# A linear-attention and gated-unit kernel in float32: plain out products for two batches, another load order, a new plan

## The chip, the cores and the metric

The kernel runs on one core of one Trainium2 chip. The metric is device time in microseconds; the time before is the median of three runs, and the profile is of one further execution.

## The reference

Eight batches, eight heads, 576 tokens, head size 64. All arithmetic is float32; three weights arrive as float64 and are narrowed on the chip.

```python
kv = np.einsum('bhsd,bhse->bhde', k, v)
out = np.einsum('bhsd,bhde->bhse', q, kv)
rms = np.sqrt(np.mean(out * out, axis=-1, keepdims=True) + 1e-06)
x = out / rms * g_norm                      # then (B,H,S,D) -> (B,S,512)
for t in range(5):
    gate_pre += conv_w[t] * xp[:, t:t + S, :]   # causal taps over tokens
gate = 1.0 / (1.0 + np.exp(-gate_pre))
return (gate * (x @ w_val)) @ w_out
```

## The kernel before, in words

The work goes batch by batch, and each batch has five stages.

**Attention.** `kv_product` (L400) makes the 64x64 products of k and v, a pair of heads to a step, from two half loads of each (`load_half`, L257) and from tails of 64 tokens (`load_tails`, L266). `kv_copy` (L415) puts them on the diagonal of `kvbd`. q has to stand with the head's elements on the partitions: the first two batches turn it on TensorE (`turn_q_rows`, L439, then `sort_q`, L452), the others on VectorE (`turn_q`, L425). `raw_product` (L478) multiplies both for one chunk of 128 tokens (a last chunk has 64). The norm is `square` on ScalarE, `sums` on VectorE, `powers` (exponent -0.5) on GpSimd and `normalise` on VectorE. x is then turned: on TensorE for the first two batches (`turn_x`, L528, `keep_x`), by VectorE and DMA for the others (`turn_blocks`, `move_blocks`).

**Gates.** Four strips of 128 channels in a batch: `gate_start` on ScalarE, four `gate_tap` (L569) on VectorE, and a sigmoid. **Val.** x @ w_val in float32: batches 0 to 3 in plain form (`val_product`, L580, 32 steps), the others in a form with seven block products in place of eight (`val_fast`, L619). `gated` multiplies val by the gate into `gv`, which has room for three batches.

**Out.** gv @ w_out, by pairs of batches (i). In a batch two groups p of two chunks of 128 tokens each use seven block products in place of eight: `fast_product` (L703) has 7 steps of two matmuls each, 128x128 by 256 columns. They need sums of weights (`weight_sums`, once) and of tokens (`token_sums`, L682, four VectorE operations for each batch), and seven `fast_keep` (L725) collect the banks: four ScalarE copies and three VectorE adds. The last 64 tokens of both batches of a pair form one chunk more, made by `out_product` (L658) in plain form with 64-wide weights, and `keep_out` (L670). `store` (L746) issues four transfers for each chunk.

**Weights.** Each of nine pieces (four of w_val, four of w_out, conv_w) is loaded (`stage_weight`) and narrowed in eight steps (`narrow_weight`), five on VectorE and three on ScalarE.

What sets the order: nothing is scheduled at run time. `Planner` (L52) is given every step with an engine, a duration, a due time (`want`), what it needs and which ring of buffers it takes; `SHIFTS` (L21) moves due times of single kinds and batches. `order` (L103) takes again and again the step that can start first, ties by due time, and the steps are recorded in that order. Each engine runs its own instructions in that order, and waits by semaphores for the others. The loads stand in SP's queue likewise: at most eight transfers are under way, since each takes one of eight semaphores in turn. Before a TensorE step of the first 60 us of the plan, `keep_warm` (L392) puts matmuls of the identity (L397) into the time that the plan has free; they write to a spare half of the bank that holds kv. The PSUM rings are kv 1, raw 2, tp 1 and mm 4 banks; `kv_copy` reads the same bank as the keep-warm matmuls write.

Of the kernel before, what the change touches and what calls it, by code (L numbers as in the profile page):

```python
# [15 lines left out]
P = 128  # L16
# [2 lines left out]


SHIFTS = {  # L21
    "fast_keep": {3: 8},
    "fast_product": {1: -15, 3: -3.5},
    "gate_tap": {0: 30, 1: 40.5, 2: 66, 3: 64, 4: 72.5, 5: 53, 6: 56, 7: 32.5},
    "kv_product": {2: 48.5, 5: 19.5},
    "load_half": {("k", 0): -105.5, ("k", 3): 4.5, ("k", 4): -12, ("k", 6): -27.5, ("v", 0): -11.5,
        ("v", 4): -13, ("v", 5): -11, ("v", 7): -9.5},
    "load_q": {2: -6, 5: 2, 6: -30, 7: -22},
    "load_q_rows": {0: -16},
    "load_tails": {4: -1.5, 5: 0.5, 7: -0.5},  # L30
    "move_blocks": {3: 22.5},
    "narrow_weight": {("wout", 1): 6, ("wout", 2): 6, ("wout", 3): 7.5, ("wval", 0): -19,
        ("wval", 1): -26.5, ("wval", 2): 14},
    "normalise": {2: 12, 7: -20},
    "out_product": {1: -28},
    "raw_product": {4: -1.5},
    "stage_weight": {("cw", 0): -102, ("wout", 1): 30.5, ("wout", 2): 7, ("wout", 3): 57, ("wval", 1): 3,
        ("wval", 2): -109, ("wval", 3): -93},
    "sums": {2: 16.5, 3: -3.5, 4: -37.5, 5: 11.5, 7: 24.5},
    "token_sums": {0: -31.5},  # L40
    "turn_blocks": {6: -13, 7: 1},
    "turn_q": {2: 16.5, 3: 11.5},
    "turn_x": {1: 11.5, 6: 14},
    "val_fast": {4: 38, 7: 9},
    "val_keep": {6: -64},
    "val_product": {0: 11, 1: 10.5, 2: 34.5, 3: 34.5},
    "val_sums": {1: 41},
    "x_sums": {6: 16},
}


# [85 lines left out]
def kernel(  # L137
# [37 lines left out]
    nc = tc.nc  # L175
    B, H, S, D = q.shape
    C = H * D
    HP = H // 2
    NJ = S // P
    SF = NJ * P  # L180
    T = S - SF
    NK = C // P
# [8 lines left out]
    TURNED = 2  # L191
    TURNED_X = 2
    FAST_VAL = range(4, B)
    GATES = 3
    GVS = 3
    assert NJ == 4 and NB == 18
# [24 lines left out]
    gv = const.tile([P, NK, GVS * S], FP32, name="gv")  # L221
# [5 lines left out]
    cw = const.tile([NK * K, P], FP32, name="cw")  # L227
    cwT = const.tile([P, K, NK], FP32, name="cwT")
    wval = const.tile([P, NK, C], FP32, name="wval")
    wout = const.tile([P, NK, C], FP32, name="wout")  # L230
# [427 lines left out]
    def out_product(i, c):  # L658

        po = ps("mm", [P, C], f"out{i}_{c}")  # L660
        for jt in range(NK):
            for r in range(2):
                first = (2 * i + r) % GVS * S + SF
                nc.tensor.matmul(  # L664
                    po[r * T:(r + 1) * T], gv[:, jt, first:first + T], wout[:, jt, :],
                    start=(jt == 0), stop=(jt == NK - 1),
                )
        st["po", i, c] = po
# [287 lines left out]
    def gated_all(*batches):  # L956
        return [("gv", (b, jt)) for b in batches for jt in range(NK)]

    def single(b, first):

        key = b // 2, 2 * NJ
        plan.add(
            "PE", 3.6, first, out_product, *key,
            needs=gated_all(b - 1, b) + [("wout", jt) for jt in range(NK)],
            gives=[("po", key)], takes=[("mm", ("po", key))], frees=[("gv", b - 1), ("gv", b)],
        )
        plan.add(
            "ACT", 0.5, first + 3.6, keep_out, *key, needs=[("po", key)], gives=[("ot", key)],
            takes=[("ot", key)], frees=[("mm", ("po", key))],
        )  # L970
        plan.add(
            "SP", 2.0, first + 4.3, store, *key, needs=[("ot", key)], frees=[("ot", key)],
            load=0.26 / RATE,
        )

    def outputs(b, first):

        i, h = divmod(b, 2)
        used = gated_all(b)
        for n in range(4):  # L980
            plan.add(
                "DVE", 0.62, first - 4.0 + n, token_sums, i, h, n,
                needs=used + ([("sums", (i, h, n - 1))] if n else []), gives=[("sums", (i, h, n))],
                takes=[("w64", ("sums", i, h, n // 2))] if n % 2 == 0 else [],
            )
        for m in range(2):
            p = 2 * h + m
            t = first + 6.2 * m
            for n in range(7):
                key = i, p, n  # L990
                last = (i, p, n - 1) if n else (i, p - 1, 6) if p else None
                own = {2: 0, 4: 2, 5: 1, 6: 4}.get(n)
                own_sums = {1: 0, 2: 1, 4: 2, 5: 3}.get(n)
                plan.add(
                    "PE", 0.9, t + 0.88 * n, fast_product, *key,
                    needs=used + ([("fast", last)] if last else [])
                    + ([("kept", (i, p, own))] if own is not None else [])
                    + ([("sums", (i, h, own_sums))] if own_sums is not None else [])
                    + ([("wsum", 3)] if n not in (0, 3) else [("wout", jt) for jt in range(NK)]),
                    gives=[("fast", key)],  # L1000
                    takes=[(out_bank(i, p), (bank, i, p)) for bank in ("cb", "a")] if n == 0 else [],
                    frees=([("gv", b)] if n == 6 and m else [])
                    + ([("w64", ("sums", i, h, 0))] if n == 2 and m else [])
                    + ([("w64", ("sums", i, h, 1))] if n == 5 and m else []),
                )
                chunk = i, 2 * p + n
                plan.add(
                    "DVE" if n in (3, 4, 5) else "ACT", 0.37 if n in (3, 4, 5) else 0.29,
                    t + 0.88 * n + 0.9, fast_keep, *key,
                    needs=[("fast", key)]  # L1010
                    + [("kept", (i, p, k)) for k in ((), (), (), (0,), (1,), (2, 3), ())[n]],
                    gives=[("kept", key)],
                    takes=[("ot", chunk)] if n < 2 else [],
                    frees={5: [(out_bank(i, p), ("cb", i, p))], 6: [(out_bank(i, p), ("a", i, p))]}.get(n, []),
                )
            for r, parts in enumerate(((3, 5), (4, 6))):
                chunk = i, 2 * p + r
                if b == B - 1 and m:
                    last_stores(chunk, r, t + 6.8)
                    continue  # L1020
                plan.add(
                    "SP", 2.0, t + 6.8, store, *chunk, needs=[("kept", (i, p, n)) for n in parts],
                    frees=[("ot", chunk)], load=0.26 / RATE,
                )
        if h:
            single(b, first + 12.4)
# [9 lines left out]
    def loads_kv(b, want):  # L1036
        for i in range(2):
            for name, src in (("k", k), ("v", v)):
                plan.add(
                    "SP", 0.5, want, load_half, name, src, b, i, gives=[(name, b, i)],  # L1040
                    takes=[(f"{name}{i}", b)], load=0.52 / RATE, ahead=0.0,
                )
            if i == 0:
                plan.add(
                    "SP", 1.3, want, load_tails, b, gives=[("tails", b)], takes=[("tails", b)],
                    load=0.36 / RATE, ahead=0.0,
                )

    def loads_q(b, want):
        if b < TURNED:  # L1050
            for i in (2, 0, 1):
                plan.add(
                    "SP", 0.6, want, load_q_rows, b, i, gives=[("q", b, i)], takes=[("q", (b, i))],
                    load=(0.52 if i < 2 else 0.2) / RATE, ahead=0.0,
                )
        else:
            for hp in range(HP):
                plan.add(
                    "SP", 2.4, want + 0.1 * hp, load_q, b, hp, gives=[("q", b, hp)],
                    takes=[("q", (b, hp))], load=0.56 / RATE, ahead=0.0,  # L1060
                )
# [19 lines left out]
    weight(("cw", 0), 0.0, 0.1, 0.1)  # L1081
    plan.add("PE", 0.3, 5.0, turn_cw, needs=[("cw", 0)], gives=["cwps"], takes=[("tp", "cw")])
    plan.add("DVE", 0.3, 5.5, keep_cw, needs=["cwps"], gives=["cwT"], frees=[("tp", "cw")])
    begin = 27.0
    loads_q(0, 0.1)
    loads_kv(0, 0.2)
    attention(0, 15.0, 1.9, 10.0, 7.0)
    for jt in range(NK):
        weight(("wval", jt), 0.3 + 0.01 * jt, 16.0 + (4.0, 8.0, 20.0, 28.0)[jt], 0.5)
    gates(0, 28.0, 4.5)  # L1090
    products(0, begin, 3.4)
    loads_kv(1, 0.4)
    loads_q(1, 0.5)
    attention(1, 40.0, 2.2, 34.0, 37.0)
    begin += NK * NV * 3.4
    gates(1, begin - 1.0, 4.5)
    for jt in range(NK):
        weight(("wout", jt), 0.6 + 0.01 * jt, begin + 1.0 + 4.6 * jt, 0.57)
    for n in range(4):
        plan.add(  # L1100
            "DVE", 0.61, begin + 20.0 + n, weight_sums, n,
# [58 lines left out]
```

## Time and profile before

| | before |
|---|---|
| time, median of 3 (lowest, highest) | 333.29 us (333.08, 333.42) |
| span of the profiled execution | 331.6 us |
| mean granted TensorE clock | 0.98 |
| float32 taps (L571) on VectorE | 128, 98.7 us busy |
| plain val (L583) on TensorE | 256 records, 66.3 us busy |
| single out (L664) on TensorE | 64 records, 14.6 us busy |
| token sums (L697) on VectorE | 32, 673 to 684 ns each |
| adds of `fast_keep` (L730) on VectorE | 48, 413 to 420 ns each |
| traffic | 55.36 MB, mean 167 GB/s |

Engine names in the profile: PE is TensorE (PEld its weight loads), DVE is VectorE, ACT is ScalarE, POOL is GpSimd, SP is the queue that issues transfers. A float32 matmul has two records. A duration of a record overlaps with the next, so the distance from one start to the next is what a step costs. In an answer by stretch, the columns are the stretch, its length, busy time and number of instructions for PE, PEld, DVE, ACT and POOL, the granted clock, the busy share of DMA and GB/s. In a group's row, the numbers behind the first bar are busy us and mean ns of one, then idle time before it. In a timeline row they are start and length in us.

### The profile page before, as it was taken

What the parts mean: (1) busy time and instruction counts of PE and PEld (TensorE: products, weight loads), DVE (VectorE), ACT (ScalarE), POOL (GpSimd) and SP (SyncE); (2) the same over time, 40 slices, a digit from 0 to 9 for tenths busy, and PEclk for the clock granted to TensorE, in tenths of its full rate; (3) what the DMA queues carried; (4) which work ended last, traced back from release to release, by engine and by line L of the source; (5) the groups of instructions that cost most, each with busy time, mean ns of one, the idle gap of its engine ahead of it and who ended that gap; (6) DMA issues with size and microseconds to landing.
All of it is one profiled execution on the core that took longest, in us unless ns stands there. A gap on an engine that the chain in (4) does not pass through costs nothing.

```text
span 331.6 us, 6348 instructions
## 1 busy us (share of the span) xinstructions
PE 316.0 (95%) x2221; PEld 254.1 (77%) x2221; DVE 279.1 (84%) x504; ACT 150.5 (45%) x325; POOL 137.1 (41%) x178
## 2 busy tenths in 40 slices
PE   4599999999999999999999999999999999999993
PEld 4598878878888588878886887888878578888761
DVE  1626988999999999998989989997999999988610
ACT  1639769584235355334425344434444343443211
POOL 3006604615384749777103154959162682000000
PEclk9599999999999999999999999999999999999998
DMA  6999979686399679899867856516410034202223
GB/s 207 321 262 349 255 179 312 172 250 194 107 229 277 183 212 231 230 229 249 218 154 238 239 133 189 161 34 154 101 34 0 25 89 111 64 2 63 63 64 95
DMA packets 46013, 55.36 MB, mean 167 GB/s; under 512 B 15754, under 2 KB 36254, under 8 KB 45982
## 3 DMA queue, kind: packets, MB, share of 16 engines
q1 hardware_dynamic: 42558, 48.41, 53.9%
q0 software_dynamic: 3072, 6.30, 8.4%
q8 instruction: 17, 0.28, 0.4%
q10 hardware_dynamic: 352, 0.26, 0.3%
q14 instruction: 14, 0.11, 0.1%
HBM read 39.21 MB, written 9.44 MB: 147 GB/s over the span
## 4 chain that ended last, share of the span: by engine, by line
PE 88%; DVE 4%; DMA 3%; ACT 1%; issue 1%; SPq 1%; DVEq 0%
PE val L583 19%; PE a L721 15%; PE cb L721 12%; PE raw L485 10%; PE va L633 9%; PE kv L408 6%; PE vc L633 4%; PE out L664 4%; DMA q<-in_q_dram 3%; PE qTps L446 3%; PE vb L633 2%; PE kv L397 2%; PE xTps L531 2%; DVE gate L571 1%; DVE gv L596 1%
## 5 line engine op out<-in xcount | busy, mean ns | idle before, releaser
L513 POOL TENSOR_TENSOR rt<-ss,mhalf 128x8 f32<-128x8 f32 (+1 forms) x40 | 67.5, 1693 | 119.7 <-DVE ss L507 119.6
L571 DVE SCALAR_TENSOR_TENSOR gate<-xT,cwT,gate 128x576 f32<-128x576 f32 x128 | 98.7, 808 | 1.7 <-ACT gate L565 1.6
L583 PE MATMUL val<-xT,wval 128*128 128x288 f32 x256 | 66.3, 408 | 0.0
L554 POOL DMA_DIRECT2D xT<-y x96 | 52.8, 557 | 14.6 <-DVE ss L507 4.8
L583 PEld LDWEIGHTS val<-xT,wval 128*128 128x128 f32 x256 | 47.5, 190 | 11.8
L485 PEld LDWEIGHTS raw<-kvbd,qT 128*128 128x128 f32 (+1 forms) x320 | 35.3, 180 | 6.5 <-issue 4.3
L485 PE MATMUL raw<-kvbd,qT 128*128 128x128 f32 (+1 forms) x320 | 39.1, 280 | 0.3 <-ACT kvbd L418 0.3
L499 ACT ACTIVATE sq<-raw 128x512 f32<-128x512 f32 (+1 forms) x40 | 22.1, 553 | 27.4 <-PE raw L485 26.3
L721 PE MATMUL a<-wsum,sums 128*128 128x256 f32 x128 | 33.3, 382 | 0.7 <-ACT ot L732 0.6
L730 DVE TENSOR_TENSOR ot<-cb,ot 128x256 f32<-128x256 f32 x32 | 13.5, 420 | 19.0 <-PE cb L721 10.3
L592 ACT COPY gv<-val 128x288 f32<-128x288 f32 x32 | 12.7, 397 | 35.1 <-PE val L583 34.8
L507 DVE TENSOR_REDUCE ss<-sq 128x8 f32<-128x520 f32 (+1 forms) x40 | 25.0, 625 | 3.3 <-ACT sq L499 3.2
L721 PEld LDWEIGHTS a<-wsum,sums 128*128 128x128 f32 x128 | 23.8, 190 | 5.1 <-ACT ot L732 1.3
L596 DVE TENSOR_TENSOR gv<-gv,gate 128x576 f32<-128x576 f32 x32 | 23.6, 750 | 3.1 <-ACT gate L578 1.3
L521 DVE TENSOR_TENSOR x<-raw,rt 128x512 f32<-128x512 f32 (+1 forms) x40 | 24.9, 625 | 0.6 <-POOL rt L513 0.5
L565 ACT ACTIVATE gate<-xT,cwT 128x576 f32<-128x576 f32 x32 | 23.4, 769 | 3.0 <-DVE gv L596 2.7
L578 ACT ACTIVATE gate<-gate 128x576 f32<-128x576 f32 x32 | 21.4, 682 | 5.8 <-DVE gate L571 5.3
L408 PEld LDWEIGHTS kv<-v,k 128*64 128x64 f32 x512 | 17.6, 137 | 4.4 <-issue 3.5
L408 PE MATMUL kv<-v,k 128*64 128x64 f32 x512 | 20.5, 225 | 0.0
L633 PE MATMUL va<-xs,vsum 128*128 128x288 f32 x64 | 18.1, 406 | 0.0
L721 PE MATMUL cb<-wsum,sums 128*128 128x256 f32 x64 | 16.8, 386 | 0.3 <-DVE sums L697 0.3
L721 PE MATMUL a<-wsum,gv 128*128 128x256 f32 x64 | 16.8, 386 | 0.1
(106 smaller groups left out, 506.1 us busy)
## 6 DMA issues: line engine op xcount, KB each, us to landing
q<-in_q_dram SPq DMA_DIRECT2D x96, 140.0 KB, 4.6
out_dram<-ot SPq DMA_DIRECT2D x140, 64.0 KB, 1.8
k<-in_k_dram SPq DMA_DIRECT2D x16, 512.0 KB, 7.4
v<-in_v_dram SPq DMA_DIRECT2D x16, 512.0 KB, 5.4
xT<-y POOLq DMA_DIRECT2D x96, 64.0 KB, 3.0
w_wval<-in_moe_w_val_dram SPq DMA_DIRECT2D x4, 512.0 KB, 7.1
q<-in_q_dram SPq DMA_DIRECT2D x4, 512.0 KB, 8.3
w_wout<-in_moe_w_out_dram SPq DMA_DIRECT2D x4, 512.0 KB, 9.2
```

Source lines behind the costliest of these rows:

```text
L408: nc.tensor.matmul(kvp[r * D:(r + 1) * D, hp, :], st["k", b, half][:, h, j, :] if j < NJ else kl[:, 2 * hp + r, :], st["v", b, half][:, h, ...
L485: nc.tensor.matmul(raw[row * m:(row + 1) * m, col * P:(col + 1) * P], st["qT", b][:, hp, c * P:c * P + m], kv_bd[b % 2][:, hp, :], start=T ...
L507: nc.vector.reduce_sum(out=ss[:, 0:n], in_=st["sq", b, c][:, 0:n], axis=AX.X)
L513: nc.gpsimd.tensor_tensor(out=rt[:, 0:n], in0=st["ss", b, c][:, 0:n], in1=mhalf[:, 0:n], op=ALU.pow)
L521: nc.vector.tensor_tensor(out=x[:, 0:n * D].rearrange("p (h e) -> p h e", h=n), in0=st["raw", b, c][:, 0:n * D].rearrange("p (h e) -> p h ...
L554: nc.gpsimd.dma_start(out=xTs[b % 2][i * TB:(i + 1) * TB, :, first:first + P], in_=y[a * TB:(a + 1) * TB, i])
L565: nc.scalar.activation(out=gate[:], in_=xTs[b % 2][:, jt, HALO:SX], func=AF.Copy, scale=cwT[:, K - 1, jt:jt + 1])
L571: nc.vector.scalar_tensor_tensor(out=gate[:], in0=xTs[b % 2][:, jt, tap * TB:tap * TB + S], scalar=cwT[:, tap, jt:jt + 1], in1=gate[:], op ...
L583: nc.tensor.matmul(val[:], wval[:, kc, jt * P:(jt + 1) * P], xTs[b % 2][:, kc, HALO + n * SV:HALO + (n + 1) * SV], start=(kc == 0), stop=( ...
L596: nc.vector.tensor_tensor(out=both, in0=both, in1=st["gate", b, jt][:], op=ALU.mult)
L633: nc.tensor.matmul(st[bank, "val", b, mj][:], weights_[:, k], tokens()[:, k], start=(n in (0, 1, 3) and k == 0), stop=(k == NK // 2 - 1), ...
L721: nc.tensor.matmul(st[bank, i, p], tokens()[:, k], weights_[:, k], start=(n < 2 and k == 0), stop=(k == NK // 2 - 1), skip_group_check=True)
```

## The change

Three edits. First, the eight chunks of 128 tokens of batches 0 and 1 are no longer made by `fast_product`: for batches outside `FAST_OUT = range(2, B)` `out_product` makes each chunk by four matmuls of 128x128 by 512 columns, `keep_out` copies it by one ScalarE operation, and no token sums are needed. That takes one bank at a time in place of two. Second, the loads of the opening are in another order: conv_w and the first piece of w_val, then the tails of k and v, then q, another piece of w_val, then k and v of batch 0 (before: a piece of w_val, k, conv_w, another piece of w_val, q, v, tails). Third, all due times are set anew (`SHIFTS`, `begin`, the times of `attention`, `weight` and `gates` at the start), so that the order of nearly all steps differs. In TensorE's queue, kv of batches 2, 3 and 4 now stands in one block each, and five more val products stand ahead of raw of batch 2; 34 keep-warm matmuls stand where 30 did, none of them at the very start.

```diff
 SHIFTS = {
...
-    "kv_product": {2: 48.5, 5: 19.5},
+    "kv_product": {1: -67, 7: -2.5},
-    "load_half": {("k", 0): -105.5, ("k", 3): 4.5, ("k", 4): -12, ("k", 6): -27.5, ("v", 0): -11.5,
-        ("v", 4): -13, ("v", 5): -11, ("v", 7): -9.5},
+    "load_half": {("k", 0): -22, ("k", 3): 1, ("k", 6): 8.5, ("k", 7): 9, ("v", 0): -6, ("v", 3): 0.5,
+        ("v", 4): -11.5, ("v", 5): -12.5, ("v", 6): -9},
-    "load_q_rows": {0: -16},
-    "load_tails": {4: -1.5, 5: 0.5, 7: -0.5},
+    "load_q_rows": {0: -88.5, 1: 15.5},
+    "load_tails": {0: -105, 1: -4.5, 2: 18.5, 3: 0.5, 4: -0.5, 7: -13},
-    "stage_weight": {("cw", 0): -102, ("wout", 1): 30.5, ("wout", 2): 7, ("wout", 3): 57, ("wval", 1): 3,
-        ("wval", 2): -109, ("wval", 3): -93},
+    "stage_weight": {("cw", 0): -265.5, ("wout", 3): 58, ("wval", 0): -147, ("wval", 3): -34.5},
...
+    FAST_OUT = range(2, B)
...
         po = ps("mm", [P, C], f"out{i}_{c}")
         for jt in range(NK):
+            if c < 2 * NJ:
+                first = (2 * i + c // NJ) % GVS * S + c % NJ * P
+                nc.tensor.matmul(
+                    po[:], gv[:, jt, first:first + P], wout[:, jt, :],
+                    start=(jt == 0), stop=(jt == NK - 1),
+                )
+                continue
...
+        if b not in FAST_OUT:
+            for c in range(NJ):
+                plain(i, h * NJ + c, first + 3.45 * c, 3.47, used, [("gv", b)] if c == NJ - 1 else [])
+            if h:
+                single(b, first + 12.4)
+            return
...
-    begin = 27.0
-    loads_q(0, 0.1)
-    loads_kv(0, 0.2)
-    attention(0, 15.0, 1.9, 10.0, 7.0)
+    begin = 28.0
+    loads_q(0, 0.01)
+    loads_kv(0, 0.04)
+    attention(0, 18.0, 1.8, 10.0, 5.0)
     for jt in range(NK):
-        weight(("wval", jt), 0.3 + 0.01 * jt, 16.0 + (4.0, 8.0, 20.0, 28.0)[jt], 0.5)
-    gates(0, 28.0, 4.5)
+        weight(("wval", jt), 0.09 + 0.01 * jt, 16.0 + 3.0 * jt, 0.5)
+    gates(0, 34.0, 4.5)
     products(0, begin, 3.4)
-    loads_kv(1, 0.4)
-    loads_q(1, 0.5)
-    attention(1, 40.0, 2.2, 34.0, 37.0)
+    loads_q(1, 0.14)
+    loads_kv(1, 0.2)
+    attention(1, 38.0, 2.2, 34.0, 28.0)
```

## The prediction

> **What bounds the kernel now.** I read the page first: busy shares, the slices, the chain. TensorE (PE) and VectorE (DVE) are both nearly full, and PE carries the chain that ends last.
>
> ```profile
> PE 316.0 (95%) x2221; PEld 254.1 (77%) x2221; DVE 279.1 (84%) x504; ACT 150.5 (45%) x325; POOL 137.1 (41%) x178
> ...
> PE 88%; DVE 4%; DMA 3%; ACT 1%; issue 1%; SPq 1%; DVEq 0%
> ```
>
> Then the busy times by stretch: 0 to 12 and 12 to 20 us are the opening, 81 to 126 the outputs of batches 0 and 1, 265 on the end. PE is idle in the first only; in the second it runs at a lower clock.
>
> ```profile
> 0.00:12.00 12.00, 3.73 (x18) 3.54 (x18) 2.77 (x22) 3.52 (x6) 2.61 (x10) 0.83 0.81 235
> 12.00:20.00 8.00, 7.96 (x77) 7.58 (x79) 5.75 (x13) 4.49 (x11) 0.00 (x0) 0.62 1.19 270
> ...
> 81.00:126.00 45.00, 44.85 (x367) 35.39 (x366) 43.62 (x78) 17.47 (x38) 27.36 (x33) 1.00 0.70 194
> ```
>
> The timeline of PE in the opening: q is turned from 17.45, kv runs at 22.26, raw at 26.07; between them stand keep-warm matmuls (L397), the first 18 records at 230 ns each.
>
> ```profile
> 12.04 1.12 PE L446 MATMUL qTps<-ident,q 64*64 64x64 f32 x16 [6.95 <-DMA q<-in_q_dram]
> 13.31 4.21 PE L397 MATMUL kv<-ident 128*128 128x128 f32 x18
> 17.45 4.01 PE L446 MATMUL qTps<-ident,q 128*64 128x128 f32 x64
> 22.26 0.69 PE L408 MATMUL kv<-v,k 128*64 128x64 f32 x16
> 26.07 4.42 PE L485 MATMUL raw<-kvbd,qT 128*64 128x128 f32 x40
> ```
>
> Last, PE's groups by shape and its timeline inside the out stage: a fast step (4 records) takes 0.86 us from start to start (97.60 to 98.46), but 0.96 from 95.77 to 96.73, where the step that followed had a semaphore to wait for.
>
> ```profile
> L583 PE MATMUL val<-xT,wval 128*128 128x288 f32 x256 | 66.3, 408 | 0.0
> L721 PE MATMUL a<-wsum,gv 128*128 128x256 f32 x64 | 16.8, 386 | 0.1
> L664 PE MATMUL out<-wout,gv 128*64 128x512 f32 x64 | 14.6, 597 | 0.0
> ```
>
> ```profile
> 95.77 1.13 PE L721 MATMUL a<-wout,gv 128*128 128x256 f32 x4
> 96.73 1.03 PE L721 MATMUL cb<-wsum,sums 128*128 128x256 f32 x4
> 97.60 1.03 PE L721 MATMUL a<-wsum,sums 128*128 128x256 f32 x4
> 98.46 1.03 PE L721 MATMUL cb<-wout,gv 128*128 128x256 f32 x4
> ```
>
> From these I make one balance. Let V be the start of the second val product of batch 0 (43.14 us); both kernels have by then done the same steps (q, kv, raw, turns of batch 0; q and kv of batch 1; one val). PE's work after V, at start-to-start times: 31 val at 1.94, 56 fast val at 0.97, 112 fast out at 0.865, 4 single out at 3.44, raw of seven batches at 4.15, kv of six at 2.36, turns 3.3: 271.7 us. The last matmul ends at 326.05, so 326.05 - 43.14 - 271.7 = 11.2 us are waits, most of them 0.1 us each. By stretch (starts against shortest durations): 1.6 to 81 us, 2.7 to 126, 2.4 to 200, 1.7 to 265, 2.8 after. The stores then take 5.5 us.
>
> **What the Trainium skill says.** "TensorE: Matmul & The Clock Gate", Back-to-back issue gap, gives N / 2.4 + 2.5 ns for a warm matmul. The trace has two records to a float32 matmul (256 for 128 val matmuls); if a record is two passes, 256 columns give 2 x 256 / 2.4 + 2.5 = 216 ns, and the trace has 0.865 / 4 = 216. Its section on the HAM clock gate says that PE runs at half rate until about 3.4 us of sustained work in a free-running window; the trace agrees: granted 0.62 from 12 to 20 us, 230 ns keep-warm records there and 110 later. The section Step-by-step says PE pulls weight loads ahead of running matmuls; the 0.1 us at fresh waits fits that, though no run here shows the cause. "DMA: Bandwidth & Descriptors", Why small descriptors are slow, bears on the 128 KB tails: about 0.75 us each by their landings, against 1.3 to 1.6 for most 512 KB halves.
>
> **The change, part by part.**
>
> *Plain chunks.* 28 fast steps go: 28 x 0.865 = 24.2 us. 8 plain chunks come, each 4 matmuls of 128x128 weights over 512 columns, 8 records. No row shows that: twice the 256-column record gives 8 x 2 x 0.216 = 3.46 us, the skill's price 8 x 429 ns = 3.43, and the single out (L664, twice as many half-wide matmuls in pairs) takes 3.44 to 3.58. I take 3.44: 27.5 us; the ends are 27.4 and 28.6. PE: +3.3 us, all on its path.
>
> DVE loses 8 token sums (0.68) and 12 adds (0.42): 10.4 us busy, 8.8 by spacing. ACT loses 16 copies of 0.37 and gains 8 of 0.59, nothing at 45% busy. The stores are the same.
>
> *Opening.* The transfers land one after another; issue plus time to landing gives, before, q halves at 13.3 and 14.8, v at 16.3 and 18.8, tail of k at 19.2, tail of v between 19.2 and 20.7 (estimate 19.9). After, exactly the same transfers stand ahead of the second v half, so it lands at 19.9 (estimate); but the tails and q go first, q by about 8.6 and 10.1. Conv weights are first: narrowed 2.6 us after landing (9.4 to 12.0 before), so PE starts near 6.2, turns the q tail at 7.4, then 10 keep-warms at 0.46 (4.14 / 9) while cold, turns q in 3.94: done at 16 to 17.6 by the clock's window. 12 keep-warms of 0.22 fill to 19.4 (18.6 to 20.3). kv: two steps, a keep-warm, and two that need v at 19.9: ends at 22.1 (21.4 to 23.0), against 24.7. Three keep-warms now wait behind the copy of kv (0.9 us) and cost 0.7, so raw starts at 23.8 instead of 26.07. From raw to V before: 17.1 us. The same steps follow, plus the turn of batch 1's q tail (0.75, it stood ahead of raw), less one keep-warm: 17.7. The norms are ready in time: the second x takes 6.2 us from raw's start and PE gets there at 6.4. k and v of batch 1 land at 37.6 in both, behind the same bytes. V = 41.5: 1.6 us gained, 0.7 to 2.5.
>
> *Replanned order.* The waits after V. Up to 81: kv of batch 2 is one block, not two, and five val products stand ahead of raw of batch 2, where 0.45 was lost: 1.6 becomes 1.1. Out stage: the fast steps held 1.0 of the 2.7, kv of batches 3 and 4 fall in one block each: 1.4. 126 to 200: DVE's sums now come long before PE asks (queue sums put DVE's lead 10 us and more ahead of before's): 2.0. Then 1.7 as before, and 2.4 for 2.8 at the end, with one 0.75 wait unlikely to recur. Sum 8.6 for 11.2.
>
> What waits behind what: raw of batch 2 needs four q transposes, last of a DVE queue of 33.4 us after the first gate tap (22 taps at 0.73, 3 gate products, 5 sums, 5 norms, 14 weight steps, 4 transposes). The tap follows at 41.2, so 75.5 with 0.9 for waits; PE arrives 33.7 + 1.1 after V, at 76.3. It fits by 0.8 us; behind it stand all of PE's steps. The other moves I cost at nothing: by the same landings and queue sums their inputs are there 2 us or more ahead.
>
> Sum: 41.5 + (271.7 + 3.3) + 8.6 = 325.1, against 326.05; with the same tail the span falls by 1.0 and 333.3 becomes 332.3.
>
> **The rivals.** (1) *Even*: the opening gains 1.6 but the waits only 1.5, since most 0.1 us waits are on ACT and DMA and the plan is still dense: -1.6 + 3.3 - 1.5 = +0.2, 333.5. For it: of 197 steps after V that wait on a semaphore by the program's order, 131 start on time already; little is left to free. (2) *Slower*: PE is the bound and gets 3.3 us more; the cold clock or the second v holds kv to 23.0 (gain 0.7), the new order brings waits of its own (1.1 saved): +1.5, 334.8; one hand-over as tight as the q transposes missed by a microsecond adds that. For it: PE busy 20.00 of 20 in most stretches. Against: DVE, the other full engine, is relieved just there.
>
> **How the numbers follow.** Forecast 0.45, even 0.25, slower 0.30. Low end: gain 2.5 and waits 7.6, so -2.5 + 3.3 - 3.6 = -2.8: 330.5. High: gain 0.7 and waits 10.6, so -0.7 + 3.3 - 0.6 = +2.0: 335.3. Less than 2 in 10 is left outside, most of it above. Faster by over 0.2% is the forecast, same the first rival, slower the second.
>
> **What would show it.** raw of batch 0 at 23.8 and V at 41.5; plain chunks 3.44 apart; DVE near 270 busy; waits after V near 8.6; the last matmul near 325. Wrong if V comes at 42.5 or later, if raw of batch 2 waits for DVE, or if PE shows gaps over 1 us after 130.

## The result, and the profile after

The changed kernel takes 334.57 us (median of 4 runs, 334.43 to 334.67), the kernel before 333.35 (333.08 to 333.42). The ratio is 1.0038, with a 95% interval of 1.002 to 1.0055: slower by 1.2 us, where 1.0 us faster was forecast. A second comparison gave 334.25 against 333.43 us, 1.0029 (1.0016 to 1.0043).

The page of the changed kernel, its busy times and the engine line of its chain:

```profile
PE 318.8 (96%) x2181; PEld 245.0 (74%) x2181; DVE 272.1 (82%) x484; ACT 149.5 (45%) x317; POOL 133.5 (40%) x178
...
PE 94%; DMA 1%; DVE 1%; ACT 1%; SPq 1%; issue 0%; DVEq 0%; ACTq 0%
```

VectorE fell from 279.1 to 272.1 us, as meant. TensorE's busy time rose by 2.8 us, and it carries 94% of the chain of work that ended last, where it carried 88%: the kernel has become more purely bound by TensorE. The busy times by stretch (length, then PE, PEld, DVE, ACT and POOL, granted clock, DMA share, GB/s) say the same:

```profile
0.00:12.00 12.00, 5.20 (x34) 4.77 (x35) 6.06 (x29) 5.08 (x9) 2.68 (x10) 1.00 0.85 238
12.00:20.00 8.00, 8.00 (x101) 7.59 (x102) 1.31 (x3) 4.54 (x15) 0.00 (x0) 1.00 1.16 299
81.00:126.00 45.00, 45.00 (x324) 28.04 (x323) 36.40 (x65) 15.47 (x30) 30.03 (x36) 1.00 0.74 209
```

From 81 to 126 us VectorE works 36.4 us where it worked 43.6, and TensorE is busy for 45.00 of 45 us, where it was for 44.85. There was no idle time for the relief to remove; what the balance called waits lies inside these busy 45 us, between the starts of steps.

The plain chunks have a group of their own, and TensorE's timeline shows their spacing:

```profile
L664 PE MATMUL out<-wout,gv 128*128 128x512 f32 x64 | 28.7, 594 | 0.0
```

```profile
84.85 3.60 PE L664 MATMUL out<-wout,gv 128*128 128x512 f32 x8
88.28 1.05 PE L485 MATMUL raw<-kvbd,qT 128*128 128x128 f32 x8
89.17 3.60 PE L664 MATMUL out<-wout,gv 128*128 128x512 f32 x8
```

From 84.85 to the start of the next step, 88.28, are 3.43 us; 3.44 was forecast. The prediction had taken that from the single out chunk; doubling the 216 ns of a 256-column record gives 3.46.

Last, TensorE's timeline in the opening:

```profile
13.27 3.71 PE L446 MATMUL qTps<-ident,q 128*64 128x128 f32 x64
16.91 2.94 PE L397 MATMUL kv<-ident 128*128 128x128 f32 x24
19.78 0.69 PE L408 MATMUL kv<-v,k 128*64 128x64 f32 x16
...
21.10 0.49 PE L397 MATMUL kv<-ident 128*128 128x128 f32 x2
...
23.75 0.94 PE L397 MATMUL kv<-ident 128*128 128x128 f32 x6 [0.84 <-ACT kvbd L418]
24.61 1.64 PE L485 MATMUL raw<-kvbd,qT 128*64 128x128 f32 x15
```

q is turned 4 us earlier than before, from 13.27 and not from 17.45. But raw of batch 0 starts at 24.61, only 1.5 us earlier, and between the end of q and raw stand 16 keep-warm matmuls (32 records of L397).

The same balance as in the prediction, by the starts in both traces. V is the start of the second val product of batch 0, in the timelines of before and of after:

```profile
43.14 4.15 PE L583 MATMUL val<-xT,wval 128*128 128x288 f32 x16
...
42.20 4.15 PE L583 MATMUL val<-xT,wval 128*128 128x288 f32 x16
```

The waits are the time from V to the end of the last matmul, less TensorE's work:

| us | before | forecast | after |
|---|---|---|---|
| V | 43.14 | 41.5 | 42.20 |
| TensorE's work after V | 271.7 | 275.0 | 275.0 |
| waits after V | 11.2 | 8.6 | 10.7 |
| last matmul ends | 326.05 | 325.1 | 327.87 |
| tail to the end of the span | 5.53 | 5.5 | 4.91 |

So the span's +1.2 us is -0.94 (V) +3.3 (work) -0.5 (waits) -0.6 (tail), rounded. It is the difference of one pair of profiles. The time of an execution is longer than its span, by 2.16 us in the kernel before and by 1.79 in the kernel after (means of the 20 and 10 executions of the second comparison); why this part differs, the traces don't show.

### The profile page after: what moved, and what is told of

Its sections match the earlier page's. It is cut to its first block, busy times and chain, and to the rows that moved or that the text cites. A ratio compares the mean times of both kernels' runs of the same rounds, so it can differ in the third digit from the quotient of the medians.

```text
span 332.8 us, 6209 instructions
## 1 busy us (share of the span) xinstructions
PE 318.8 (96%) x2181; PEld 245.0 (74%) x2181; DVE 272.1 (82%) x484; ACT 149.5 (45%) x317; POOL 133.5 (40%) x178
## 4 chain that ended last, share of the span: by engine, by line
PE 94%; DMA 1%; DVE 1%; ACT 1%; SPq 1%; issue 0%; DVEq 0%; ACTq 0%
PE val L583 19%; PE a L728 12%; PE raw L485 10%; PE cb L728 10%; PE va L633 10%; PE out L664 8%; PE kv L408 6%; PE vc L633 5%; PE out L671 4%; PE kv L397 3%; PE qTps L446 3%; PE vb L633 2%; PE xTps L531 2%; DMA q<-in_q_dram 1%; SPq L268 0%; DVE ot L737 0%
## 5 line engine op out<-in xcount | busy, mean ns | idle before, releaser
L554 POOL DMA_DIRECT2D xT<-y x96 | 53.0, 558 | 17.7 <-DVE sums L704 4.2
L664 PE MATMUL out<-wout,gv 128*128 128x512 f32 x64 | 28.7, 594 | 0.0
L728 PE MATMUL a<-wsum,sums 128*128 128x256 f32 x96 | 25.1, 383 | 0.0
L408 PEld LDWEIGHTS kv<-v,k 128*64 128x64 f32 x512 | 17.6, 138 | 4.9 <-issue 4.0
L679 ACT COPY ot<-out 128x512 f32<-128x512 f32 x12 | 7.0, 585 | 31.4 <-PE out L664 22.1
L664 PEld LDWEIGHTS out<-wout,gv 128*128 128x128 f32 x64 | 11.7, 190 | 12.1 <-issue 11.5
L737 DVE TENSOR_TENSOR ot<-cb,ot 128x256 f32<-128x256 f32 x24 | 10.1, 419 | 12.3 <-ACT ot L741 9.5
L728 PEld LDWEIGHTS a<-wsum,sums 128*128 128x128 f32 x96 | 17.8, 190 | 3.1 <-ACT ot L739 0.4
```

Source lines behind the costliest of these rows:

```text
L408: nc.tensor.matmul(kvp[r * D:(r + 1) * D, hp, :], st["k", b, half][:, h, j, :] if j < NJ else kl[:, 2 * hp + r, :], st["v", b, half][:, h, ...
L554: nc.gpsimd.dma_start(out=xTs[b % 2][i * TB:(i + 1) * TB, :, first:first + P], in_=y[a * TB:(a + 1) * TB, i])
L664: nc.tensor.matmul(po[:], gv[:, jt, first:first + P], wout[:, jt, :], start=(jt == 0), stop=(jt == NK - 1),)
L728: nc.tensor.matmul(st[bank, i, p], tokens()[:, k], weights_[:, k], start=(n < 2 and k == 0), stop=(k == NK // 2 - 1), skip_group_check=True)
```

## The experiments

The theories. **1**: TensorE is the bound, each pair of batches with plain chunks costs it about 2.9 us, and relief of VectorE gives nothing back. **2**: relief of VectorE is worth the 1.3 to 2.6 us of waits that were forecast, and the new order behind V lost it again. **3**: what the opening gains is lost at later hand-overs. **5**: the keep-warm matmuls of the opening stand in the way of kv and raw. Theory 4 belongs to one run alone and is in its expectation.

Several of these kernels have the order of all steps written out, one line for each, in place of the planner, so that only what is named moves:

```diff
-        for start, step in plan.order():
-            ...
+        for line in STEPS.split("\n"):
+            what = tuple(line.split())
+            if what[0] == "keep_warm":
+                keep_warm(int(what[1]))
+            else:
+                step = steps[what]
+                step["fn"](*step["args"])
```

In the tables of results, "work" is TensorE's work after V by the prices of the prediction, and "waits" what is left of the time from V to the last matmul.

### Plain chunks alone, in the old order

```diff
 STEPS of the kernel before:
-fast_product 0 0 0
...
-fast_product 0 0 4
+out_product 0 0
...
+out_product 0 1
...
-token_sums 0 0 0
-fast_keep 0 0 3
```

> The order of all steps is that of the kernel before, written out step for step, with its opening; only the 28 fast steps of batches 0 and 1 are exchanged for 8 plain chunks, each chunk at the place of the first and the fifth of its pair's seven steps; the 8 token sums and the 12 additions leave VectorE's queue and nothing else moves. Theory 1 (TensorE is the bound, relief of VectorE gives it nothing): V stays at 43.1, TensorE's work after V grows by 3.3 us, the waits fall by no more than 0.5 (those of the fast steps themselves), so +2.8: 336.1 us. Theory 2 (the relief of VectorE is worth what was forecast, 1.3 to 2.6 us of waits, and the new order gave it away): +0.7 to +2.0: 334.0 to 335.3 us.

Measured: 335.23 us against 333.48, ratio 1.0062 (1.0044 to 1.0079). V 41.98, 285.77 us from V to the last matmul: 2.87 more than before (282.90), so +3.3 of work and -0.4 of waits. Theory 1 had this number. By its time alone the run would fit theory 2 (334.0 to 335.3 us); it is lower than theory 1 said because V came at 41.98 in this profile, though nothing in the opening had been changed, and because the part of the time outside the span is 0.4 us shorter here too. More on V below.

### The double dose

```diff
-    FAST_OUT = range(2, B)
+    FAST_OUT = range(4, B)
```

with the order of before, and the steps of batches 0 to 3 exchanged as above.

> The first run with a double dose: plain chunks in the place of the fast steps of batches 0 to 3, all else in the order of the kernel before; TensorE gets 6.6 us more, VectorE 20.8 us less. Theory 1 (TensorE is the bound and pays each pair of batches with 2.87 us from V on): 282.9 + 5.7 = 288.6 us from V to the last matmul, 338 to 339 us. Theory 2 (with enough relief VectorE gives something back): 286.5 us or less from V on, 336.5 us or less.

Measured: 338.80 us against 333.12, ratio 1.0157 (1.0136 to 1.0178). 289.00 us from V on, 6.1 more than before, against 5.7 by theory 1 and 3.6 by theory 2. The page shows VectorE at 78% and TensorE still at 96%:

```profile
PE 321.8 (96%) x2125; PEld 235.8 (70%) x2125; DVE 263.5 (78%) x464; ACT 147.7 (44%) x309; POOL 137.9 (41%) x178
```

The second pair of batches costs 3.2 us where the first cost 2.87: more relief of VectorE brings no more back.

### The relief alone

```diff
-        total = lambda s: lambda: st["sums", i, h, s // 2][:, s % 2, :, m, :]
+        total = lambda s: lambda: wout[:, EVEN, m * P:(m + 1) * P] if i == 0 else st[
+            "sums", i, h, s // 2][:, s % 2, :, m, :]
 STEPS of the kernel before:
-token_sums 0 0 0
...
-fast_keep 0 0 3
```

> The kernel before with its order and its fast steps on TensorE, but VectorE without the 8 token sums and the 12 additions of batches 0 and 1: 10.4 us less of VectorE's work, TensorE's instructions the same (the fast steps read slices of the output weights where they read the token sums, and the additions are left out, so the outputs of batches 0 and 1 are partial). It measures by itself what relief of VectorE is worth. Theory 1: TensorE's waits fall by 0.5 us at most: 332.8 to 333.3 us. Theory 2: by 1.3 to 2.6 us: 330.7 to 332.0 us.

Measured: 332.67 us against 333.48, ratio 0.9976 (0.9962 to 0.9989). VectorE's busy time fell to 271.9 us, the same relief as the change gives; TensorE's went from 316.0 to 316.2:

```profile
PE 316.2 (96%) x2221; PEld 254.6 (77%) x2221; DVE 271.9 (82%) x484; ACT 150.4 (45%) x325; POOL 137.0 (41%) x178
```

From V to the last matmul are 282.75 us against 282.90. The relief by itself takes 0.15 us off TensorE's path; theory 2 wanted 1.3 at least. The rest of the timed 0.8 us lies in part outside the span (1.78 us in the mean here, 2.15 in the kernel before), in part ahead of V (42.76 in this profile), where the edit changes no step; the part on V below says what moves V.

### A VectorE that is half idle

```diff
-        total = lambda s: lambda: st["sums", i, h, s // 2][:, s % 2, :, m, :]
+        total = lambda s: lambda: wout[:, EVEN, m * P:(m + 1) * P]
 STEPS of the kernel before:
-gate_tap 0 0 3
...
-token_sums 0 0 0
...
-fast_keep 0 0 3
```

> The kernel before in its order, with all of TensorE's steps, but VectorE without any gate tap, token sum or addition of the out stage (the fast steps read slices of the output weights in place of token sums; the outputs are not those of the reference): VectorE's busy time falls from 279 to about 135 us. It shows what of the 11.2 us of waits behind V a free VectorE could take away at all. Theory 1 (most of them are hand-overs that cost 0.1 us each whoever gives and however early): 8.5 to 10 us stay, 280.2 to 281.7 us from V to the last matmul, 331 to 332.5 us. Theory 2 (TensorE waits because VectorE is late): 3 to 6 us stay, 275 to 278 us from V on, 325 to 329 us.

Measured: 330.69 us against 332.94, ratio 0.994 (0.992 to 0.996). The busy times of the page, and the stretch of the out stage:

```profile
PE 314.7 (96%) x2221; PEld 255.4 (78%) x2221; DVE 154.5 (47%) x296; ACT 149.2 (45%) x325; POOL 127.9 (39%) x178
```

```profile
81.00:126.00 45.00, 44.81 (x367) 35.60 (x366) 24.50 (x45) 17.45 (x38) 24.92 (x32) 1.00 0.72 199
```

VectorE fell to 154.5 us (135 was the estimate). With 125 us less of its work, TensorE needs 280.30 us from V on, where it needed 282.90. So 8.6 of the 11.2 us of "waits" are left when VectorE is idle for half the time: they aren't time in which TensorE waits for VectorE's throughput. That 8.6 is also what the forecast gave to a change which took 7 us from VectorE, not 125. It had spent all that a free VectorE could give. By the prediction's own sums over stretches 2.0 of the 2.6 us that it gave back lie behind 265 us, and 0.1 in the out stage of batches 0 and 1 (81 to 126 us), which is where the change relieves VectorE. The view of waits lists TensorE's idle times, engine and line against releaser (us in total, times, longest); its first two lines, the opening's waits for q and for the identity, are left out here:

```profile
PE raw L485 <- ACT kvbd L418: 0.3, 1, 0.3
PE kv L397 <- ACT kvbd L418: 0.2, 1, 0.2
PE a L728 <- ACT ot L743: 0.2, 1, 0.2
PE a L728 <- ACT ot L739: 0.2, 1, 0.2
```

None of these is VectorE. What the 8.6 us consist of, many hand-overs of about 0.1 us by the spacing of starts, was not tested singly.

### The new opening with the old order, in two attempts

Steps up to V as in the kernel after, the later ones as in the kernel before; first with fast steps everywhere, then with plain chunks for batches 0 and 1.

> All steps up to V in the order of the kernel after (its loads, its keep-warm matmuls), all later steps in the order of the kernel before, all eight batches with fast steps. Theory 1: V comes at 42.2 as after, 0.9 earlier, and the rest follows it on TensorE: 332.4 us. Theory 3 (what the opening gains is lost again at the next hand-overs, which are set by VectorE's queue or the landings of batch 1): raw of batch 2 waits 0.9 longer, 333.3 us.

> The opening of the kernel after up to V and plain chunks for batches 0 and 1, but all other steps behind V in the order of the kernel before: against the kernel after only the replanned order behind V is missing. Theory 1: the parts add up, -0.9 and +2.8: 335.2 us, so that the new order is worth -0.6 of the 334.6 of the kernel after. Theory 2 (the new order has brought waits of its own): 333.2 to 334.4 us, faster than the kernel after.

Measured: 341.49 us (1.024, 1.0221 to 1.0259) and 343.06 us (1.0291, 1.0268 to 1.0313). Neither theory: the join was at fault. V was 42.46 and 42.20, as expected, but a wait of 5.6 and 5.1 us stood ahead of raw of batch 1. VectorE's timeline of the first shows why:

```profile
43.17 0.69 DVE L356 SCALAR_TENSOR_TENSOR wout<-ot_wout,wexp_wout 128x512 f32<-128x512 f32 x1
49.15 0.71 DVE L431 STREAM_TRANSPOSE qT<-q 128x512 f32<-128x512 f32 x1 [5.28 <-DMA q<-in_q_dram]
```

The old order has the first transpose of batch 2's q here, the new opening hadn't loaded those rows yet, and every later step of VectorE's queue stood behind it. The mended pair loads the rows behind the last k and v of batch 1 and puts the transpose next to the second one:

```diff
+load_q 2 0
+load_tails 2
 stage_weight wout 1
...
-turn_q 2 0
...
+turn_q 2 0
 turn_q 2 1
```

> The second run with the opening of the kernel after and all later steps of the kernel before, fast steps in all batches; it mends the join of the second run, which set the transpose of batch 2's first q rows at the head of VectorE's queue before these rows had been loaded: the load of these rows and of batch 2's tails now stands behind the last k and v of batch 1, and the transpose next to the second one. Theory 1 (the opening is worth what V gains, TensorE carries it to the end): V 42.2, time from V to the last matmul 282.9 as in the kernel before, 332.4 us. Theory 3 (the gain is lost again at later hand-overs): V 42.2, but 283.8 us from V to the last matmul, 333.3 us.

> The same mended join, with plain chunks for batches 0 and 1 at the places of the fast steps; against the kernel after only its new order behind V is missing. Theory 1 (the new order behind V is worth nothing, up or down): V 42.2, 285.7 us from V to the last matmul as in the kernel after and as in the first run, 334.5 us. Theory 2 (the new order has brought waits of its own that eat the relief): 284 us from V on, 333 us. Theory 4 (the new order saves some waits, only fewer than forecast): 286.2 or more, 335.2 us.

Measured: 333.93 us against 332.94, ratio 1.0028 (1.0013 to 1.0042), and 336.81 us, ratio 1.0112 (1.0095 to 1.013). V 41.53 and 42.56; from V to the last matmul 283.89 and 286.28 us, which is 1.0 and 0.5 us more than the same steps take behind the old opening (282.90 and 285.77). In both, transposes of x (at 66.9 and 67.9 us) wait 0.7 us for ScalarE, which stands at a gate whose taps come late from VectorE's queue; the moved transpose of q is in that queue, which fits, but was not tested by itself. So up to 1 us comes back as waits behind this join. It isn't what theory 3 said, a gain that is lost because V comes early: with V 3 us earlier still and the same join, the stretch behind V is no longer (283.73 us at V 38.47, in the last run below). In time the opening with all its keep-warms, joined to the old order, is no gain: 1.0 us slower, as much as the longer stretch behind V.

Against the kernel after, the second of the pair lacks only the new order behind V. It is 0.6 us longer from V on, of which the join is 0.5 (286.28 against 285.77 behind the old opening). So the new order hardly changes TensorE's waits: 285.66 in the kernel after, 285.77 with the old order. Neither theory 2 nor theory 4 is needed.

### Fewer keep-warm matmuls

```diff
 STEPS of the kernel after:
-keep_warm 12
+keep_warm 6
 kv_product 0 0
...
-keep_warm 1
 kv_product 0 2
...
-keep_warm 3
+keep_warm 1
 raw_product 0 4
```

> The kernel after, step for step, but with 6 keep-warm matmuls ahead of kv of batch 0 where it has 12, none between its two halves where it has one, and one behind the copy of kv where it has three. Theory 1 for the opening (the keep-warms are in the way of kv and raw, since v has landed at 18.9): kv ends 1.7 us earlier, raw of batch 0 starts at 22.6 to 23.4 instead of 24.6, and V comes 0.6 to 1.2 earlier: 333.6 us. Rival (V is set by the chain of norms on ScalarE, VectorE and GpSimd behind raw, or the clock falls again without them): V stays within 0.3, 334.3 to 335 us.

Measured: 331.91 us against 332.94, ratio 0.997 (0.9956 to 0.9984). V came at 39.52, 2.7 us earlier than in the kernel after and more than twice what was expected, and 285.43 us from V on carried it to the end. TensorE's timeline:

```profile
16.59 1.60 PE L397 MATMUL kv<-ident 128*128 128x128 f32 x12
18.13 0.69 PE L408 MATMUL kv<-v,k 128*64 128x64 f32 x16
...
19.93 0.64 PE L408 MATMUL kv<-v,k 128*64 128x64 f32 x16
...
21.52 0.49 PE L397 MATMUL kv<-ident 128*128 128x128 f32 x2 [0.84 <-ACT kvbd L418]
21.94 4.43 PE L485 MATMUL raw<-kvbd,qT 128*64 128x128 f32 x40
```

The whole chain moved: kv by 1.65 us, raw by 2.67. To exclude that the two had been timed beside different runs, both ran again side by side (the edit takes away 9 matmuls, not 10 as the text has it):

> The kernel after itself, once more, beside the kernel before on this chip. If its V is 42.0 to 42.6 again and the time from V to the last matmul 285.7, the opening is worth 0.1 to 1.0 us by profile and the time is 1.0 to 1.5 us above that of before: 334.3 to 334.8 us. If V of the first profile was late by chance, V is 41.5 or earlier here and the time 333.8 us or less.

> The seventh run again, on the same chip as the kernel after: 10 keep-warm matmuls less ahead of raw of batch 0, all else the same. If they are the cause of the small gain of the opening, V is 2.5 to 2.8 us earlier than in the run beside it and so is the end: 331.6 to 332.2 us. If the seventh run was lucky in its landings, the difference is 1.5 us or less.

Measured: 334.25 us (1.0029) and 332.40 us (0.997, 0.9959 to 0.9981). V 42.66 and 40.24, from V on 285.42 and 285.60 us. V gains 2.4 us, a little under the range, and the end 1.9: nine keep-warm matmuls are the difference between slower and faster than before.

### No keep-warm matmuls

```diff
-keep_warm 10
-keep_warm 12
-keep_warm 1
-keep_warm 3
-keep_warm 5
-keep_warm 2
```

> The kernel after, step for step, with only the first of its keep-warm matmuls and none of the later 33 in the opening. Theory 5 taken to its end: the q rows are turned from 10.7, kv starts when v has landed (16.6 and 18.9), ends at 20.1 as in the seventh run, and V is 39.0 to 39.6: 331.4 to 332 us. Rival (without them TensorE idles 1 to 2 us and its clock falls): the granted clock in 16 to 24 us is at 0.6 to 0.8, kv and raw run at twice the time, V 41 or later, 333.5 us or more.

Measured: 331.43 us against 333.12, ratio 0.9938 (0.9915 to 0.996). V 38.55, earlier than expected, and 285.68 us from V on. TensorE's timeline:

```profile
10.86 5.80 PE L446 MATMUL qTps<-ident,q 128*64 128x128 f32 x56 [0.38 <-DMA q<-in_q_dram]
16.97 0.69 PE L408 MATMUL kv<-v,k 128*64 128x64 f32 x16 [0.32 <-DMA v<-in_v_dram]
...
18.70 0.69 PE L408 MATMUL kv<-v,k 128*64 128x64 f32 x16 [0.34 <-DMA v<-in_v_dram]
...
20.92 4.43 PE L485 MATMUL raw<-kvbd,qT 128*64 128x128 f32 x40 [0.83 <-ACT kvbd L418]
```

The turn of q runs longer (5.80 us for 56 records, where 64 take 3.71), as the rival said, but it starts earlier and ends at 16.66, where it ended at 16.98; from then on kv only waits for v, and raw runs at 4.43 us, full speed. The real work warms TensorE as well: its steps reach full pace at 16.1 us here, and at 13.3 in the last run below, which has no keep-warms either; in the kernel after they do at 13.1. And V hardly depends on it any more (38.55 and 38.47 us in these two runs), since the landing of v is what sets kv.

### The old opening with fewer keep-warms

```diff
 STEPS of the kernel before:
 keep_warm 9
 turn_q_rows 0 4
...
-keep_warm 9
+keep_warm 2
 turn_q_rows 0 3
...
-keep_warm 1
 raw_product 0 4
```

> The kernel before, step for step, but with 2 keep-warm matmuls between the q tail and the q rows of batch 0, where it has 9 (13.3 to 17.5 us), and none where one stands behind the copy of kv. Theory 5 (the keep-warms of the opening are queue time on TensorE, not only warmth): q is turned from 14.9 instead of 17.5, kv waits for the tail of v at 19.9, V comes 1.5 to 2.3 us earlier: 331.0 to 331.8 us. Rival (the clock stays low longer without them, so the turn of q and kv run longer): V within 0.4 us, 333 us.

One keep-warm more is gone, ahead of the first transpose of x. Measured: 332.82 us against 333.12, ratio 0.9987 (0.9976 to 0.9997). V 41.13, 2.0 us earlier than in the profile of before (full speed comes at about the same time in both, 18.3 and 18.1 us), but 284.00 us from V on: one wait of 0.8 us for token sums at 221 us is new. Theory 5 was right on V and wrong on the time: more than half of the 2.0 us came back behind V. What stays is a gain of 0.3 us, and the q rows were turned slowly (5.74 us for 64 records).

### Both parts that pay, without the one that costs

> The opening of the kernel after with the fewer keep-warm matmuls of the seventh run (6 ahead of kv, none within it, one behind its copy), and all later steps of the kernel before with fast steps in all batches: the two parts that paid, without the part that cost. If the parts add up: V 39.5 as in the seventh run, 283 to 284 us from V to the last matmul as in the fifth, 329.6 to 330.6 us, faster than both kernels. Rival (later steps of the order of before are set by landings, so an early V only lengthens waits): 285 us or more from V on, 331.5 us or more.

> The ninth run (opening of after, fast steps in all batches, later steps of before) without any keep-warm matmul but the first, as in the eleventh run. If TensorE carries each gain of V to the end: V 38.6, 283.9 us from V on, 328.0 us of span, 329.5 us. If an engine behind it has become the bound (the 0.7 us that the transposes of x waited at 65 us in the ninth run grow by what V gains): V 38.6, but 285 us from V on, 330.7 us as the ninth.

The edit is that of the mended opening with fast steps, with keep-warms cut as in the two runs above. Measured: 330.75 us against 333.12, ratio 0.9921 (0.9901 to 0.994), and 329.77 us against 333.43, ratio 0.9903 (0.9875 to 0.993). V 39.77 and 38.47; 283.90 and 283.73 us from V on. Both beat both kernels; the second is 3.7 us faster than before. The wait behind the join, in the first of them:

```profile
65.10 0.63 PE L531 MATMUL xTps<-ident,x 128*128 128x128 f32 x4 [0.67 <-ACT gate L578]
```

It is there in the second too, 0.7 us at 63.8, and has not grown with V: the gain beyond it reaches the end, so TensorE is still the bound.

## Why the prediction was wrong, by its own steps

| | V | from V to the last matmul | work | waits | tail |
|---|---|---|---|---|---|
| before | 43.14 | 282.90 | 271.7 | 11.2 | 5.53 |
| relief alone | 42.76 | 282.75 | 271.7 | 11.1 | 5.55 |
| VectorE half idle | 42.66 | 280.30 | 271.7 | 8.6 | 5.60 |
| chunks in the old order | 41.98 | 285.77 | 275.0 | 10.8 | 5.72 |
| chunks for four batches | 41.79 | 289.00 | 278.3 | 10.7 | 5.54 |
| after | 42.20 | 285.66 | 275.0 | 10.7 | 4.91 |
| after, again | 42.66 | 285.42 | 275.0 | 10.4 | 4.92 |
| after, fewer keep-warms | 39.52 | 285.43 | 275.0 | 10.4 | 4.94 |

**Plain chunks: right.** 3.43 us each against 3.44; +3.3 of work on TensorE, all on its path, with 0.4 of waits saved by the fast steps that went. VectorE is at 272.1 us busy, "near 270"; but the 20 operations that went are worth 7.0 us of busy time (7.2 in the relief run), where 10.4, or 8.8 by spacing, had been put down.

**Replanned order: the step that failed.** "Sum 8.6 for 11.2" measured 10.7: the relief and the new order together were to save 2.6 us of waits and saved 0.5, and plain chunks in the old order save 0.4 without any new order (10.8, first run). By stretch, with the prediction's own sums, about: 1.9 to 81 us (1.1 forecast), 1.1 in the out stage (1.4), 2.7 to 200 (2.0), 2.5 to 265 (1.7), 2.5 to the end (2.4). The out stage was even better than forecast, but not through the relief: plain chunks in the old order leave 2.3 there. What the new order takes out of this stretch comes back in the others. Of these, the prediction's reason can be tested for one: from 126 to 200 us it took VectorE's lead over TensorE ("10 us and more ahead of before's") for less waiting, and the relief runs show that a VectorE with less to do isn't: 7 us of relief are worth 0.15 us in all, 125 us are worth 2.6. For the stretch to 81 us (kv in one block, five val products ahead of raw) and the one from 200 to 265 ("as before") no run shows singly why they came out higher. The first rival's argument, that of 197 steps with a semaphore 131 start on time already, was the one to weigh more. The new order also has one wait of its own that no step had: a val product at 67.68 us waits 0.69 us for ScalarE's copy of x (idle time ahead of it, in brackets).

```profile
66.39 0.60 PE L531 MATMUL xTps<-ident,x 128*128 128x128 f32 x4
67.68 1.72 PE L583 MATMUL val<-xT,wval 128*128 128x288 f32 x6 [0.69 <-ACT xT L538]
```

**Opening: the term "raw starts at 23.8" failed too.** 1.6 us of gain measured 0.94, and about half of that in the second profile (42.66). The q rows were on time (done at 16.98 and 17.43, forecast 16 to 17.6), raw to V took 17.59 us against 17.7. But raw started at 24.61. The 12 keep-warms ended at 19.78 and not 19.4, the kv steps and the one keep-warm between them ended 0.7 later than 22.1, and the three behind the copy took 0.86 for 0.7. The prediction had kv wait for the second v half. That landed at 18.9, a microsecond before the estimate, and it bought nothing, because keep-warms and not v set kv. The prediction had listed these matmuls as filler with a price. They were the step's own bound: without nine of them V is 2.4 to 2.7 us earlier.

**One profile for V: a weakness that the prediction did not see.** V was 43.14, 42.76, 42.66, 41.98 and 41.79 in five kernels whose TensorE steps are the same up to V. The reason is when TensorE reaches full speed. In the profile of before, its steps come some 210 ns apart until 18.1 us and at about 110 from then on; the turn of q ends at 21.5 there, at 21.1 in the relief run and at 20.3 and 20.1 in the chunk runs, where full speed comes at 17.7, 15.8 and 15.6. The Trainium skill, "TensorE: Matmul & The Clock Gate", Part 1: The HAM clock gate, says that the window is free-running, so the warm point varies between runs; these traces agree, with 1.35 us between the earliest and the latest V. The new opening does the same: its six profiles (the kernel after twice, and the four of the new opening with the old order) have V from 41.53, with full speed from 11.5 us, to 42.66. The means of the two openings are 42.5 and 42.3. So a gain of 1.6 us at V was read against a single profile that lay at the late end, and the measured 0.94 is in part the luck of that pair: with all its keep-warms the new opening gains less than the profiles of one opening differ among themselves.

**The tail: not "the same".** 4.91 us against 5.53, in every kernel with the new order behind V (4.91 to 4.94) and in none with the old (5.52 or more). It is all of the kernel's gain from the new order that was found. The single out chunk of the last pair now starts at 318.47, 9.4 us ahead of the last matmul's end, and not 5.6 us ahead of it, so fewer stores are left behind it; that this is the reason was argued from the timeline, not tested.

**The q transposes of batch 2** fitted, with more room than worked out: the last is done at 76.29 us (75.5 forecast), and raw of batch 2 starts at 77.58 (76.3), without a wait above 0.2 us. So none of the three signs of being wrong came in the first profile: V was under 42.5 (42.66 in the second one), raw of batch 2 didn't wait for VectorE, and TensorE shows no gap over 0.3 us after 130. The forecast was wrong by many small waits that none of its signs watched.

**The rivals.** "Slower" was the right one, 334.8 us, and for the reason it gave: TensorE is the bound and gets 3.3 us more, V gains 0.7, waits of its own. That the number is so near is partly luck: fewer waits were saved than it said (0.5 for 1.1), and the shorter tail, which it didn't have, makes up for that. What spoke for it in the profile, TensorE busy for 20.00 of 20 us in most stretches, should have had the weight that VectorE's relief got.

## What to carry to other kernels

On an engine that is busy for the whole of a stretch, added work is paid in full, and relief of another busy engine is worth only what its waits show, here 0.15 us for 7 us of work; leave out the relieved engine's work alone once, before trading the bound engine's time for it. Count filler such as keep-warm matmuls as queue time of the engine that it keeps warm, and check whether real work warms it as well: taking 33 of them out, with the new loads and without plain chunks, made the kernel 1% faster than before. A change of a microsecond in an opening is not to be read from one profile when the clock's warm point moves it by as much.

## What the runs showed of the hardware

- The granted clock of the view by stretch didn't show the slow phase of the opening in the new kernels, nor in the two relief runs with the old opening. In the run without keep-warms it stands at 1.00 throughout, though the turn of q had steps 213 ns apart until 16.1 us and 109 ns from then on (starts in the trace):

```profile
12.00:16.00 4.00, 4.00 (x40) 4.00 (x39) 0.43 (x1) 2.64 (x10) 0.00 (x0) 1.00 1.10 348
16.00:20.00 4.00, 3.34 (x92) 2.96 (x88) 1.85 (x4) 2.05 (x7) 0.00 (x0) 1.00 1.18 278
```

The trace's record of the clock begins at 16.06 us in that run, and at 13.06 in the kernel after: for the time ahead of it the view has no reading and shows 1.00. The distance of starts is what tells the pace there. In the trace of before the record begins at 4.45 us, ahead of the slow phase, and the view has it:

```profile
7.90:18.00 10.10, 5.96 (x41) 5.58 (x43) 6.59 (x18) 5.76 (x11) 0.00 (x0) 0.50 1.16 305
```

- From the first of the opening's continuous work to the warm pace passed about 5.3 us in the kernel after (7.8 to 13.1), 6.1 before (12.0 to 18.1) and 8.0 without keep-warms (8.1 to 16.1, with one gap of 0.8 us). That is longer than one window of about 3.4 us, the figure that the Trainium skill, "TensorE: Matmul & The Clock Gate", Part 1: The HAM clock gate, gives for the free-running window, and it fits a window that doesn't start with the work: in all these traces each stretch at one clock that begins and ends within the record lasts a whole number of 3.41 us. Before, it is one at full speed from 4.45, three at half from 7.86, and full speed from 18.1. Work that starts inside such a window has warmed TensorE only at the end of a later one.
- A gap of 1.6 us (15.3 to 16.85 in the last run) did not cool TensorE: two kv steps behind it took 1.2 us, as they do elsewhere. The waits of 5.6 and 5.1 us in the two runs with the faulty join did: the clock stood at half for one window of 3.41 us from 57.5 and 57.3 us, about where these waits ended.
